# Two transformer layers on one core: the norm's root on another engine, VectorE's exp chain in halves, and other banks for the last MLP groups

## The chip, the core and the metric

The kernel runs on one core of a Trainium2 chip. A core has five engines, each with its own in-order queue: TensorE (matrix multiply, "PE" in the profile, its weight loads "PEld"), VectorE ("DVE"), ScalarE ("ACT"), GpSimd ("POOL") and SyncE ("SP", which here only starts DMAs). They work on the on-chip memory SBUF; TensorE writes its results to PSUM, eight banks of 128 partitions x 512 float32. Engines wait for each other through semaphores. The metric is the device time of one execution in microseconds (us), lower is better. Before the change it is 1762.49 us, the median of three runs (1761.7 to 1763.58).

## The reference

x is 2048 rows of 512 values in bf16. Two layers follow each other, with the same weights:

```
x = x + attention(norm(x)) @ wo        # 32 heads of 16 values, softmax over all 2048 keys
x = x + relu(norm(x) @ w1) @ w2        # w1: 512 x 1792, w2: 1792 x 512
norm(x) = (x - mean) / sqrt(var + 1e-5)
```

The attention makes 2 x 32 x 2048 x 2048 exponentials. That is 4096 blocks of 128 keys x 512 queries, and every element of them has to pass through an engine once or more.

## The kernel before

The program is written out in full by Python code that plans it: the code keeps a clock of its own for TensorE (`now_pe`), VectorE (`now_dve`) and the exponentials (`exp_end`), with constants for the cost of each operation, and by these decides in which order instructions are put into the engines' queues. Once written, the order is fixed.

**Attention.** The main loop (L1048 to 1197) makes one slot after another, 1366 in all. In a slot TensorE makes scores of three blocks (L1147) into one of two PSUM tiles `ps_s` of three banks each, and ScalarE takes the exponential of the whole tile in one instruction (L1156) into one of five buffers `e`. Later TensorE multiplies `e` with the values (`pv`, L835) and sums in the bank `ps_o`. So two slots are in flight: one tile is filled while the other is read. A segment is one head of each of four groups of partitions, for one chunk of queries; at its end VectorE copies `ps_o` out (L739, L758 or L760), and the division by the softmax sums follows over small DMAs and a broadcast `r` that GpSimd's queue starts (L787).

**Blocks that VectorE takes.** In some slots ScalarE takes only two blocks, and the third goes to VectorE, which works out the exponential from the bits of the float. Such blocks come in pairs, two slots apart. For each half VectorE does a first step that reads the scores from PSUM into `di` (L881, `first_step`, put ahead of other work as a "must"). When both halves are there, `chain` (L904) queues five steps on the pair together, 128 x 1024 elements each: `bits` into `dm`, three times `step` (L912: add a constant to one input, multiply by the other), and `bits` into `di` (L906). Then TensorE takes up the three parts of the result (`emit_pair`). At most two pairs may be open (L1071). The chain's steps have the lowest rank among VectorE's tasks (`run_dve`, L323): musts first, then the copies out of the one bank `ps_f`, then other tasks, then chain steps.

**The rest of the layers** is cut into groups that TensorE runs between slots, at a pace that the planner works out from what is left: projections for keys, values and queries, the output projection (`o_group`, L588), the MLP (`h_group`, L613; `z_group`, L644). All of these go through one bank, `ps_f` (`bank()`, L188), which VectorE empties (relu of the MLP: L622). Only before and after the main loop (`wide`) are seven banks used. w1 is loaded tile by tile into four buffers (`load_w1`, L603), four tiles ahead; each load is issued on SP when a group has used its buffer.

**The norm.** `ln_rows` (L485) queues, for a chunk of four (at the end two) row tiles, the statistics (L438, L439), then four tasks of `ln_rstd` (L441), then `ln_apply` (L468), which needs the last of them; TensorE turns the result over (`ln_transpose`) and VectorE copies it out (L513). The four tasks find 1 / sqrt(var + eps) for all rows of the chunk at once, on tiles of 128 x 4 elements: the first makes a start value from the bits of the float (L446, L449, L453), each of the other three is one Newton step of three instructions (L458, L461, L462). The planner counts 600 ns for each task. There are 15 norms of this kind; the first norm of all and the last one are written out directly (L963, L1235) and keep `ln_rstd`.

**The end.** When the last slots are done, `run_all` (L379) puts in whatever groups are left, and then a hand-written last stage (L1202 to 1297) does the last chunk of 256 rows with all banks.

Of the kernel before, what the change touches and what calls it, by code (L numbers as in the profile page):

```python
# [14 lines left out]
ACTF = mybir.ActivationFunctionType  # L15
ALU = mybir.AluOpType
# [6 lines left out]
def kernel(  # L23
# [10 lines left out]
    nc = tc.nc  # L34
# [28 lines left out]
    LEAD, C2, C1, C0 = 0.43216083424908747, -0.036015386827967774, 0.769178243088122, 0.36146642138144963  # L63
# [8 lines left out]
    FLOOR = 0.56  # L72
    C_LAG, R_LAG, U_LAG = 3600.0, 10500.0, 3000.0
    VLAG = 1
    AHEAD = (8.0, 8.0)
    LATE = 0.0
    MID = 2
# [44 lines left out]
    htp = [sb([P, 2, QS], BF16, f"ht{n}") for n in range(NF // 2)]  # L122
    ht = [htp[ft // 2][:, ft % 2, :] for ft in range(NF)]
    ot = [sb([P, QS], BF16, f"ot{t}") for t in range(NT)]
    dm = sb([P, 2, QS], FP32, "dm")
    dy = sb([P, 2, QS], FP32, "dy")
# [18 lines left out]
    va_ = [sb([P, TPC], FP32, f"va{n}") for n in range(2)]  # L145
    ya_ = [sb([P, TPC], FP32, f"ya{n}") for n in range(2)]
    ta_ = [sb([P, TPC], FP32, f"ta{n}") for n in range(2)]
    warm = sb([P, 1], FP32, "warm")

    ps_s = [psum.tile([P, W, QS], FP32, name=f"ps_s{n}") for n in range(2)]  # L150
    ps_o = psum.tile([P, QS], FP32, name="ps_o")
    ps_f = psum.tile([P, QS], FP32, name="ps_f")
# [31 lines left out]
    wide = [True]  # L184
    bank_no = [0]
    in_bank = [None]

    def bank():  # L188
        if not wide[0]:
            return ps_f[:]  # L190
        n = bank_no[0] % 7
        bank_no[0] += 1
        in_bank[0] = (2, 0) if n == 6 else (n // W, n % W)
        if n == 6:
            return ps_f[:]
        return ps_s[n // W][:, n % W, :]
# [26 lines left out]
    def mark(key, engine="dve", lag=0.0):  # L223
        made[key] = (engine, (now_pe if engine == "pe" else now_dve)[0] + lag)
# [34 lines left out]
    def task(cost, fn, makes=(), deps=(), place=None):  # L259
        t = {"cost": cost, "fn": fn, "makes": makes, "deps": deps}  # L260
        dve_q.insert(len(dve_q) if place is None else place, t)
        maker.update({k: t for k in makes})
# [60 lines left out]
    def run_dve(until, musts):  # L323

        while True:
            can = [(0, m[1], m) for m in musts[:1]]
            if now_dve[0] < until:
                can += [(1, e[1], None) for e in list(evac)[:1]]
                for t in dve_q:
                    ready = at(t["deps"], "dve")  # L330
                    if ready is not None:
                        can.append((3 if "chain" in t else 2, ready, t))
            if not can:
                return
            soon = [c for c in can if c[1] <= now_dve[0] + 40.0]
            kind, ready, x = min(soon, key=lambda c: c[0]) if soon else min(can, key=lambda c: c[1])
            if kind and ready >= until:
                if not musts:
                    return
                kind, ready, x = can[0]  # L340
            if kind == 0:
                musts.pop(0)
                dve_run(x[0], x[1])
                x[2]()
            elif kind == 1:
                do_evac()
            else:
                do_task(x)
# [30 lines left out]
    def run_all():  # L379
        while True:  # L380
            finish_group()
            g = next(
                (g for q in (urgent, work) for g in q if at(g["deps"], "pe") is not None), None
            )
            if g is not None:
                start_group(g)
            elif dve_q:
                do_task(next(t for t in dve_q if at(t["deps"], "dve") is not None))
            else:
                break  # L390
        assert not (urgent or work)
# [39 lines left out]
    def ln_n(tag):  # L431
        return ln_seq.index(tag) % 2
# [8 lines left out]
    def ln_rstd(tag, part):  # L441

        n = ln_n(tag)
        a, y, t1 = va_[n], ya_[n], ta_[n]
        if part == 0:
            nc.vector.tensor_scalar(  # L446
                out=a[:], in0=mv[n][:, :, 1], scalar1=EPS, scalar2=None, op0=ALU.add
            )
            nc.vector.tensor_scalar(  # L449
                out=t1[:].bitcast(I32), in0=a[:].bitcast(I32), scalar1=1, scalar2=None,  # L450
                op0=ALU.logical_shift_right,
            )
            nc.vector.tensor_scalar(  # L453
                out=y[:].bitcast(I32), in0=t1[:].bitcast(I32), scalar1=-1.0,
                scalar2=float(RSQRT_SEED), op0=ALU.mult, op1=ALU.add,
            )
            return
        nc.vector.scalar_tensor_tensor(  # L458
            out=t1[:], in0=y[:], scalar=-0.5, in1=y[:], op0=ALU.mult, op1=ALU.mult
        )  # L460
        nc.vector.tensor_mul(out=t1[:], in0=t1[:], in1=a[:])  # L461
        nc.vector.scalar_tensor_tensor(  # L462
            out=y[:], in0=t1[:], scalar=1.5, in1=y[:], op0=ALU.add, op1=ALU.mult
        )

    def ln_apply(tag, tt, i):
        n = ln_n(tag)
        nc.vector.tensor_scalar(  # L468
            out=xnbuf[i][:], in0=x_t[tt][:],
            scalar1=mv[n][:, i, 0:1], scalar2=ya_[n][:, i : i + 1],  # L470
            op0=ALU.subtract, op1=ALU.mult,
        )
# [12 lines left out]
    def ln_rows(tag, tt, n, i):  # L485

        if tag not in ln_seq:
            ln_seq.append(tag)
        prev = ln_seq[ln_seq.index(tag) - 1]
        if ("st", tag, i) not in made:  # L490
            task(860, lambda: ln_stats(tag, tt + i, i), [("st", tag, i)])
        if i == n - 1:
            for part in range(4):
                task(
                    600, lambda part=part: ln_rstd(tag, part), [("rs", tag, part)],
                    [("rs", tag, part - 1)] if part else each(n, "st", tag),
                )
            for k in range(n):
                task(
                    420, lambda k=k: ln_apply(tag, tt + k, k), [("xn", tag, k)],  # L500
                    [("xT", prev, k), ("rs", tag, 3)],
                )
# [20 lines left out]
    def each(n, *key):  # L523
        return [key + (i,) for i in range(n)]
# [88 lines left out]
    def h_group(l, j, ft, war):  # L613
        n = (l * NQS + j) * NF + ft
        _, a, w = columns(l, j)

        number = QS // w
        fts = range(ft, ft + number)
        made_here = [("h", l, j, f) for f in fts]

        def fin(b):
            nc.vector.tensor_scalar(  # L622
                out=htp[ft // 2][:, ft % 2 : ft % 2 + number, a : a + w],
                in0=b.rearrange("p (f q) -> p f q", f=number),
                scalar1=0.0, scalar2=None, op0=ALU.max,
            )
            for key in made_here:
                mark(key)

        def after():  # L630
            for f in range(number):
                load_w1(n + f + NW1)

        return mm_group(
            [
                (w1buf[(n + f) % NW1][:, c, :], xn2T[:, c, a : a + w])
                for f in range(number) for c in range(NDC)
            ],
            fin, made_here,
            each(w // P, "xnT", ("ln2", l, j)) + war + [("w1", n + f) for f in range(number)],  # L640
            after=after, wide_by=w, sums=number,
        )
# [64 lines left out]
    for l in range(2):  # L707
# [11 lines left out]
        for j, Ts, a, b in steps:  # L719
            for T in Ts:  # L720
                sums = acc[8 * j :] if l else acc0
# [182 lines left out]
    def chain(key, di, de):  # L904
        def bits(out, keep, put):
            nc.vector.tensor_scalar(  # L906
                out=out[:].bitcast(I32), in0=di[:].bitcast(I32), scalar1=keep,
                scalar2=put, op0=ALU.bitwise_and, op1=ALU.bitwise_or,
            )

        def step(out, x, c, y):
            nc.vector.scalar_tensor_tensor(  # L912
                out=out[:], in0=x[:], scalar=c, in1=y[:], op0=ALU.add, op1=ALU.mult
            )

        steps = (
            (690, lambda: bits(dm, 0x007FFFFF, 0x3E800000)),
            (1260, lambda: step(dy, dm, C2, dm)),
            (1260, lambda: step(dy, dy, C1, dm)),
            (1260, lambda: step(de, dy, C0, di)),  # L920
            (690, lambda: bits(di, 0x7F800000, KAPPA_BITS)),
        )
        for n, (cost, fn) in enumerate(steps):
            k = key + (n,) if n + 1 < len(steps) else key
            task(cost, fn, [k], [key + (n - 1,)] if n else [])
            maker[k]["chain"] = True
# [271 lines left out]
    while pend:  # L1198
        emit_pv()
        run_dve(0.0, musts)  # L1200
    run_all()
    wide[0] = True  # L1202
    users.clear()
    l, j = 1, NQS
    tag = ("ln2", l, j)
# [122 lines left out]
```

The softmax here doesn't subtract the row's maximum and nothing guards it: scores larger than these inputs give would overflow.

## Time and profile before

| | |
|---|---|
| time, median of three runs | 1762.49 us |
| time of the profiled run, its span | 1761.06 us, 1759.3 us |
| ScalarE: exponentials (L1156) | 1366 instructions, 1695.6 us |
| VectorE: pairs | 166: first steps (L881) 332 x 687 ns; `step` (L912) 498 x 1.21 to 1.22 us; `bits` (L906) 332 x 0.69 us |
| VectorE: Newton steps (L458, L461, L462) | 3 x 51 instructions, 160 to 162 ns each |
| TensorE: scores (L1147) | 8100 matmuls, 761.5 us |
| VectorE: relu of the MLP (L622) | 105 instructions, 687 ns each |
| granted TensorE clock | 0.998 of full speed |

A profile is of one execution. A group's row has the line, the engine, the operation, its tiles and shapes, how often it ran, the busy time in us and the mean ns of one; behind the second bar stands how long the engine was idle just before such instructions, and whom it waited for. In the lists of waits the three numbers are the total in us, how many, and the longest. In the timeline each row has the start and the length in us, and in brackets the idle time before it with the engine and line that ended it; equal instructions that follow each other are merged. Consecutive instructions of one engine may overlap a little in these records, so a sum of durations can be more than the time from the first start to the last end.

### The profile page before, as it was taken

To read this page: it belongs to the slowest core of one execution; us is meant where nothing else is said; L and a number is where in the kernel's file an instruction comes from. 1 tells how busy PE (TensorE), PEld (TensorE's weight loads), DVE (VectorE), ACT (ScalarE), POOL (GpSimd) and SP (SyncE) were. 2 spreads that over 40 slices of the span, in tenths; PEclk is the share of its full clock that TensorE was granted. 3 is DMA by queue.
4 is the path that set the end of the run, shared out by engine and by line. 5 is a ranking of instruction groups with operands and counts; after the bars stand their busy time and mean duration, and the time that the engine had idled before them with its cause. 6 is when DMAs were issued, how large, how long until landed. Compare 5 with 4: busy or idle time off the path is not lost.

```text
span 1759.3 us, 35344 instructions
## 1 busy us (share of the span) xinstructions
PE 1643.2 (93%) x15404; PEld 533.1 (30%) x15404; DVE 1481.9 (84%) x2250; ACT 1706.0 (97%) x1386; POOL 35.5 (2%) x80
## 2 busy tenths in 40 slices
PE   8998889999999999999999999999999999999997
PEld 3222222222222222222222222222222222454454
DVE  7437889999899899899798997889988888888883
ACT  7999999999999999999999999999999999999991
POOL 0000000000000000000000000000000000000000
PEclk9999999999999999999999999999999999999999
DMA  4000000110002000021000100000110011011103
GB/s 150 1 1 2 2 2 14 35 28 14 2 17 43 17 14 8 11 43 23 8 1 7 28 10 1 3 3 17 37 21 22 9 41 29 17 21 36 27 18 84
DMA packets 104268, 38.10 MB, mean 22 GB/s; under 512 B 93713, under 2 KB 101649, under 8 KB 104113
## 3 DMA queue, kind: packets, MB, share of 16 engines
q1 hardware_dynamic: 92192, 24.38, 6.0%
q0 software_dynamic: 10576, 10.16, 3.1%
q8 instruction: 120, 1.97, 0.5%
q10 hardware_dynamic: 1344, 1.31, 0.2%
q14 instruction: 36, 0.29, 0.1%
HBM read 22.54 MB, written 2.10 MB: 14 GB/s over the span
## 4 chain that ended last, share of the span: by engine, by line
ACT 82%; PE 12%; DVE 3%; issue 2%; DMA 1%; SPq 0%; ACTq 0%
ACT e L1156 82%; PE ps_s L1147 4%; PE ps_f L409 4%; PE ps_o L835 3%; DVE dy L912 1%; PE ps_s L1222 1%; DVE ht L622 1%; DMA wqkv<-in_A_wqkv_dram 0%; DVE di L881 0%; DVE de L912 0%; DVE u L760 0%; PE ps_f L1222 0%; DMA x<-in_A_x_dram 0%; PE ps_s L980 0%; DVE stats L438 0%
## 5 line engine op out<-in xcount | busy, mean ns | idle before, releaser
L1156 ACT ACTIVATE e<-ps_s 128x1536 bf16<-128x1536 f32 (+1 forms) x1366 | 1695.6, 1458 | 5.4 <-PE ps_s L1147 4.8
L1147 PE MATMUL ps_s<-q,ktp 32*128 32x512 bf16 (+1 forms) x8100 | 761.5, 355 | 86.4 <-ACT e L1156 71.5
L835 PE MATMUL ps_o<-e,vaug 128*32 128x512 bf16 (+1 forms) x4230 | 428.9, 363 | 3.0 <-DVE u L758 1.1
L1147 PEld LDWEIGHTS <-ktp 32*128 32x128 bf16 x8100 | 243.2, 92 | 605.9 <-issue 498.7
L881 DVE TENSOR_SCALAR di<-ps_s 128x512 int32<-128x512 f32 x332 | 228.1, 687 | 83.9 <-PE ps_s L1147 81.5
L835 PEld LDWEIGHTS <-vaug 128*32 128x32 bf16 x5364 | 146.2, 94 | 304.9 <-issue 279.2
L912 DVE SCALAR_TENSOR_TENSOR dy<-dm 128x1024 f32<-128x1024 f32 x166 | 202.6, 1220 | 4.1
L912 DVE SCALAR_TENSOR_TENSOR dy<-dy,dm 128x1024 f32<-128x1024 f32 x166 | 201.8, 1216 | 2.0
L912 DVE SCALAR_TENSOR_TENSOR de<-dy,di 128x1024 bf16<-128x1024 f32 x166 | 201.2, 1212 | 1.1
L409 PE MATMUL ps_f<-xn2T,w 128*128 128x512 bf16 (+1 forms) x448 | 121.4, 370 | 4.7 <-DVE ht L622 4.7
L835 PE MATMUL ps_o<-de,vaug 128*32 128x512 bf16 (+1 forms) x756 | 112.2, 356 | 5.7 <-DVE u L760 2.4
L906 DVE TENSOR_SCALAR di<-di 128x1024 int32<-128x1024 int32 x166 | 113.7, 685 | 2.7
L906 DVE TENSOR_SCALAR dm<-di 128x1024 int32<-128x1024 int32 x166 | 114.0, 686 | 0.6
L409 PE MATMUL ps_f<-w,ht 128*128 128x512 bf16 x392 | 113.9, 383 | 0.1
L409 PE MATMUL ps_f<-xnT,wqkv 128*128 128x512 bf16 (+1 forms) x312 | 91.5, 374 | 2.5 <-DVE ktp L530 1.2
L622 DVE TENSOR_SCALAR ht<-ps_f 128x512 bf16<-128x512 f32 x105 | 72.1, 687 | 23.0 <-PE ps_f L409 22.0
L570 DVE TENSOR_SCALAR q<-ps_f,qmask 128x512 bf16<-128x512 f32 (+1 forms) x94 | 62.9, 699 | 24.2 <-PE ps_f L409 23.7
L409 PE MATMUL ps_f<-wo,ot 128*128 128x512 bf16 x240 | 69.6, 383 | 1.0 <-DVE x L593 1.0
L835 PE MATMUL ps_o<-di,vaug 128*32 128x512 bf16 (+1 forms) x378 | 70.5, 363 | 0.0
L787 POOL DMA_DIRECT2D r<-u x45 | 33.1, 736 | 1663.5 <-DVE di L881 558.8
L409 PEld LDWEIGHTS <-w 128*128 128x128 bf16 x448 | 34.2, 97 | 74.4 <-issue 58.6
L773 DVE SCALAR_TENSOR_TENSOR ot<-u,mask,r 128x512 bf16<-128x512 f32 (+2 forms) x74 | 49.4, 672 | 1.0
(85 smaller groups left out, 553.0 us busy)
## 6 DMA issues: line engine op xcount, KB each, us to landing
w<-in_B_w_dram SPq DMA_DIRECT2D x126, 128.0 KB
r<-u POOLq DMA_DIRECT2D x32, 256.0 KB, 7.1
out_dram<-x SPq DMA_DIRECT2D x16, 128.0 KB
x<-in_A_x_dram SPq DMA_DIRECT2D x14, 128.0 KB
w<-in_B_w_dram SPq DMA_DIRECT2D x1, 1792.0 KB
r<-u POOLq DMA_DIRECT2D x13, 128.0 KB, 4.5
wqkv<-in_A_wqkv_dram ACTq DMA_DIRECT2D x2, 512.0 KB
c<-u SPq DMA_DIRECT2D x56, 8.0 KB
```

The source lines that it names most:

```text
L409: nc.tensor.matmul(out, lhsT, rhs, start=i % k == 0, stop=i % k == k - 1)
L570: return nc.vector.tensor_scalar(out=qbuf[n % 2][e][:, 0:w], in0=b, scalar1=qmask[e][:, 0:1], scalar2=None, op0=ALU.mult,)
L622: nc.vector.tensor_scalar(out=htp[ft // 2][:, ft % 2 : ft % 2 + number, a : a + w], in0=b.rearrange("p (f q) -> p f q", f=number), scalar1 ...
L773: nc.vector.scalar_tensor_tensor(out=ot[t][:, at_column + a : at_column + a + w], in0=u[:, a : a + w], scalar=mask[e][:, 0:1], in1=r[:, a ...
L787: nc.gpsimd.dma_start(out=r[:, 0:width], in_=bass.AP(tensor=sums.tensor, offset=sums.offset, ap=[list(sums.ap[0]), [0, 32], [1, width]],),)
L835: nc.tensor.matmul(ps_o[32 * g : 32 * g + 32, 0 : sg["w"]], vaug[sg["l"]][kb][:, 4 * sg["T"] + g, 2 * e : 2 * e + 32], rhs, start=g not in ...
L881: first = nc.vector.tensor_scalar(out=di[:, half, :].bitcast(I32), in0=src, scalar1=EXP_BIAS, scalar2=0.0, op0=ALU.add, op1=ALU.max,)
L906: nc.vector.tensor_scalar(out=out[:].bitcast(I32), in0=di[:].bitcast(I32), scalar1=keep, scalar2=put, op0=ALU.bitwise_and, op1=ALU.bitwise_or,
L912: nc.vector.scalar_tensor_tensor(out=out[:], in0=x[:], scalar=c, in1=y[:], op0=ALU.add, op1=ALU.mult)
L1147: nc.tensor.matmul(b[:, a : a + sg["w"]], kt[32 * g : 32 * g + 32, kc : kc + P], qbuf[sg["n"] % 2][sg["e"]][32 * g : 32 * g + 32, 0 : sg[" ...
L1156: ex = nc.scalar.activation(out=eb[:, 0 : place[m]], in_=b[:, 0 : place[m]], func=ACTF.Exp, scale=1.0 / (LOG2E * UNIT),)
L1222: uses(nc.tensor.matmul(out, lhsT, rhs, start=first, stop=last), b, needs=needs)
```

## The change

Three edits are made together.

1. *The norm's root.* Where `ln_rows` queued four tasks, it queues one. It makes the start value on VectorE as before (`ln_rstd(tag, 0)`) and then issues the three Newton steps on GpSimd (`ln_newton`), four instructions a step, twelve in all, each of which needs the one before. The planner counts 600 ns of VectorE for it, and takes the result to be there 5000 ns later (`RSTD_LAG`).
2. *The chain of a pair.* Each of the three `step` instructions on 128 x 1024 elements becomes two on 128 x 512, first half and second half in turn. The planner counts 660 ns for each instead of 1260 ns for the whole. `bits` stays as it is.
3. *The groups left at the end.* While `run_all` puts in what is left after the last slot (`ending`), `bank()` goes around three banks, `ps_f` and the first bank of each `ps_s`, and the MLP's relu is done by ScalarE instead of VectorE.

```diff
+    RSTD_LAG = 5000.0
...
     def bank():
+        if ending[0]:
+            bank_no[0] += 1
+            return (ps_f[:], ps_s[0][:, 0, :], ps_s[1][:, 0, :])[bank_no[0] % 3]
         if not wide[0]:
             return ps_f[:]
...
+    def ln_newton(tag):
+
+        n = ln_n(tag)
+        a, y, t1 = va_[n][:], ya_[n][:], ta_[n][:]
+        for _ in range(3):
+            nc.gpsimd.tensor_mul(out=t1, in0=y, in1=y)
+            nc.gpsimd.tensor_mul(out=t1, in0=t1, in1=a)
+            nc.gpsimd.tensor_scalar(
+                out=t1, in0=t1, scalar1=-0.5, scalar2=1.5, op0=ALU.mult, op1=ALU.add
+            )
+            nc.gpsimd.tensor_mul(out=y, in0=y, in1=t1)
...
-            for part in range(4):
-                task(
-                    600, lambda part=part: ln_rstd(tag, part), [("rs", tag, part)],
-                    [("rs", tag, part - 1)] if part else each(n, "st", tag),
-                )
+
+            def rstd():
+                ln_rstd(tag, 0)
+                ln_newton(tag)
+                mark(("rs", tag, 3), lag=RSTD_LAG)
+
+            task(600, rstd, [("rs", tag, 3)], each(n, "st", tag))
...
+            if ending[0]:
+                nc.scalar.activation(out=out, in_=sums, func=ACTF.Relu)
+            else:
+                nc.vector.tensor_scalar(
+                    out=out, in0=sums, scalar1=0.0, scalar2=None, op0=ALU.max
+                )
...
-            (1260, lambda: step(dy, dm, C2, dm)),
-            (1260, lambda: step(dy, dy, C1, dm)),
-            (1260, lambda: step(de, dy, C0, di)),
+            (660, lambda: step(dy[:, 0], dm[:, 0], C2, dm[:, 0])),
+            (660, lambda: step(dy[:, 1], dm[:, 1], C2, dm[:, 1])),
+            (660, lambda: step(dy[:, 0], dy[:, 0], C1, dm[:, 0])),
+            (660, lambda: step(dy[:, 1], dy[:, 1], C1, dm[:, 1])),
+            (660, lambda: step(de[:, 0], dy[:, 0], C0, di[:, 0])),
+            (660, lambda: step(de[:, 1], dy[:, 1], C0, di[:, 1])),
...
+    ending[0] = True
     run_all()
-    wide[0] = True
+    ending[0], wide[0] = False, True
```

More of the change, by code (lines that the diff above doesn't have):

```diff
@@ L186 @@
     in_bank = [None]
+    ending = [False]
     def bank():
+        if ending[0]:
+            bank_no[0] += 1
+            return (ps_f[:], ps_s[0][:, 0, :], ps_s[1][:, 0, :])[bank_no[0] % 3]
         if not wide[0]:
@@ L621, in fin @@
         def fin(b):
[L622 to L626, printed above, removed]
+            out = htp[ft // 2][:, ft % 2 : ft % 2 + number, a : a + w]
+            sums = b.rearrange("p (f q) -> p f q", f=number)
+            if ending[0]:
[4 more added lines that the diff above has]
+                )
             for key in made_here:
@@ L912, in step @@
             nc.vector.scalar_tensor_tensor(
-                out=out[:], in0=x[:], scalar=c, in1=y[:], op0=ALU.add, op1=ALU.mult
+                out=out, in0=x, scalar=c, in1=y, op0=ALU.add, op1=ALU.mult
             )
```

## The prediction

> **What bounds the kernel now.** I read the page from the top (busy shares, then the chain that ended last), then the groups with shapes kept apart, the waits, and last the timeline of the end.
>
> ```profile
> PE 1643.2 (93%) x15404; PEld 533.1 (30%) x15404; DVE 1481.9 (84%) x2250; ACT 1706.0 (97%) x1386; POOL 35.5 (2%) x80
> ACT 82%; PE 12%; DVE 3%; issue 2%; DMA 1%; SPq 0%; ACTq 0%
> ```
>
> ScalarE is busy for 97% of the span and makes 82% of the last chain. GpSimd does nearly nothing. In the groups:
>
> ```profile
> L1156 ACT ACTIVATE e<-ps_s 128x1536 bf16<-128x1536 f32 x1033 | 1456.2, 1563 | 3.6 <-PE ps_s L1147 3.1
> L1156 ACT ACTIVATE e<-ps_s 128x1024 bf16<-128x1024 f32 x332 | 374.5, 1136 | 1.8 <-PE ps_s L1147 1.7
> L881 DVE TENSOR_SCALAR di<-ps_s 128x512 int32<-128x512 f32 x332 | 228.1, 687 | 83.9 <-PE ps_s L1147 81.5
> L912 DVE SCALAR_TENSOR_TENSOR dy<-dm 128x1024 f32<-128x1024 f32 x166 | 202.6, 1220 | 4.1
> ```
>
> The exponentials run from 16.66 us to 1717.3 us. From start to start in the trace, one of three blocks takes 1.330 us at the median, one of two 0.904 us: a block that VectorE takes saves ScalarE 0.426 us, a pair 0.85 us. At these medians the 1366 exponentials would take 1673.7 us from first start to last; they take 1700.0. So 26.3 us are lost in late scores, though the idle column shows only 5.4 us (an exponential overlaps the next, so a late start hides in it). The span is 16.7 us of start, 1673.7 of exponentials, 26.3 of lateness, and 42 us from the last exponential to the end. Each edit must change one of these four, or the number of pairs (166).
>
> Who makes scores late? The waits:
>
> ```profile
> PE ps_s L1147 <- ACT e L1156: 71.5, 217, 0.7
> PE ps_o L835 <- DVE u L760: 3.2, 7, 0.9
> PE ps_s L1147 <- DVE di L881: 2.4, 5, 0.8
> ```
>
> TensorE waits mostly for ScalarE itself. All its waits for VectorE between 150 and 1717 us add to some 15 us. Going back from each exponential over 60 ns late to the last wait of TensorE before it, 5.6 of the 26.3 us follow a wait for VectorE. The end:
>
> ```profile
> 1719.48 1.03 PE L409 MATMUL ps_f<-xn2T,w 128*128 128x256 bf16 x8 [0.78 <-DVE ht L622]
> 1719.48 0.75 PEld L409 LDWEIGHTS <-w 128*128 128x128 bf16 x7 [0.96 <-issue]
> 1720.55 0.69 DVE L622 TENSOR_SCALAR ht<-ps_f 128x512 bf16<-128x512 f32 x1 [1.12 <-PE ps_f L409]
> 1720.60 0.10 PEld L409 LDWEIGHTS <-w 128*128 128x128 bf16 x1 [0.37 <-DMA w<-in_B_w_dram]
> 1721.30 1.03 PE L409 MATMUL ps_f<-xn2T,w 128*128 128x256 bf16 x8 [0.78 <-DVE ht L622]
> ```
>
> Seven MLP groups stand behind the last exponential, from 1717.65 to 1729.58: eight matmuls, then TensorE waits 0.78 us for VectorE to empty the one bank, 1.82 us a group. The weight load of the group after next has only just landed (fourth line).
>
> **What the skill says.** *SBUF — State Buffer*, "Who interferes with whom": a VectorE instruction with two SBUF inputs, or in a 2-port mode, excludes a GpSimd instruction that reads SBUF, and the reverse; the later one waits for the whole of the other. The chain's steps (L912) have two SBUF inputs. No row of before shows GpSimd arithmetic, so the trace neither confirms nor denies it. *VectorE: DVE Perf Modes*, "The DRAIN you can't avoid": the next instruction waits until the pipe is empty. The trace differs: where the next doesn't depend on the one before, it starts 0.083 us before that one's end; where it does, 0.034 us after. The measurement decides. *ScalarE: Activation LUTs*, "Table sets": relu is in every set, so no table load; the trace agrees (Exp, Relu and copies, one ACT_TABLE_LOAD).
>
> **The change, part by part.**
>
> *Newton.* Nine VectorE instructions leave each of 15 norms, 0.196 us from start to start: 1.76 us each. Three lie before 50 us, where VectorE is idle enough; 12 lie among the pairs: 21 us. In the planner's costs it is 1800 ns, 21.6 us in 12 norms. GpSimd gets 12 dependent instructions. Bounds for one: below, the 0.122 us of GpSimd's memset (1.5 us in all); above, a whole half step in front of each, 0.68 + 0.12 us (9.6 us). I take 0.36: 0.12 of its own, 0.05 for the semaphore, and 0.19 for the lock (chain work is about 4.9 of the 9.4 us from pair to pair, 166 in 1556 us, and the mean rest of a half step 0.34 us). That is 4.3 us, under the 5.0 us the planner leaves, so normally hidden by the chain work placed between. Where it isn't, xn (L468) waits at the head of VectorE's in-order queue, behind it first steps, copies and evacuations, and behind these TensorE. GpSimd's queue also carries the 45 broadcasts r (L787, 0.7 us each, waiting for small DMAs), behind one of which Newton may stand, and which may stand behind Newton. I take +0.5 us in all, bounds 0 and +14.
>
> *Half steps.* A 128x1024 step takes 1.22 us, 1.067 of it for the elements at 0.96 per ns, so 0.153 is fixed; a half step is estimated at 0.686 (an addition of 128x512 f32, L758, takes 0.682). Alternating halves don't depend on the instruction just before, so each should cost 0.60: six make 3.61 us. Now three make 3.52 (1.216 each, less 0.043, the mean of the two kinds of gap as counted). So +0.09 us a pair, 15 us, which the 21 us from Newton cover. In the planner's costs a chain rises from 5160 to 5340: 180 ns x 166 = 29.9 us. Net for the plan: 29.9 - 21.6 = 8.3 us more VectorE work, at 6720 a pair 1.2 pairs fewer: +1.0 us. (The plan is limited by VectorE: in the timeline a chain begins as the last ends, and only two pairs may be open.) Bounds: 5 pairs either way, since the order is replanned, 4.3 us each way. The gain: a copy or first step that arrives during a chain step waits at the mean half of it, 0.34 instead of 0.61 us, 44% less. Of the 5.6 us of lateness behind VectorE: -2.5 us; bounds 0 and -5.6.
>
> *The end.* With three banks TensorE no longer waits for the evacuation. ScalarE has been idle there since 1717.3; its relu of 128x512 at about 0.6 us (a copy takes 0.585) fits beside a group. But w1 has four buffers, two per group: the load into group 2's first buffer, started when it had been read, released the weights of group 4 at 1722.40, 2.92 us after group 2 began at 1719.48. So two groups can't take less than 3.0 us. Starts at 0, 0.9, 3.0, 3.9, 6.0, 6.9, 9.0, end at 10.0 instead of 11.9: -1.9 us. Bounds 0 and -5.6 (seven at 0.9). VectorE's own last steps, now free early, gain nothing: TensorE's 17 matmuls from 1729.42 fill the time to ScalarE's copy at 1733.29. Against it: the norm just before. Its Newton ends at 1712.92, its transposes run at 1714.13 and 1715.00, and the second copy is done at 1715.88, 1.77 us before the first MLP group. Without chains there GpSimd's Newton takes 2 to 4 us instead of 1.77, which that slack hides; but the plan puts xn 3.2 us later (600 + 5000 against 4 x 600), perhaps behind the last exponential, where two transposes and a copy cost some 1.6 us. I take half, +0.8; bounds 0 and +3.
>
> Sum: +0.5 + 1.0 - 2.5 - 1.9 + 0.8 = -2.1 us, from 1759.3 to 1757.2 of span. The profiled run's time was 1761.06; the other runs' median is 1762.49, 3.2 above the span, so **1760.4 us**.
>
> **Rivals.** *The replanned order holds more pairs.* For: two chains in flight are the limit, and smaller steps let evacuations in sooner, so chains may start sooner. Against: the planner's VectorE cost rises by 8.3 us. Six more pairs: -5.1 us instead of +1.0, at 1754.3; I say 1755.
>
> *GpSimd is late* (slower). Place: xn after each of 12 norms in the full stretch. Point from which it decides: 5.0/12 = 0.42 us for one GpSimd instruction. At 0.8 us Newton takes 9.6; VectorE stands still after 5 us, with half the instructions left, which alone then take some 0.2 to 0.4 us each, 1.2 to 2.5 us. Scores have about one exponential, 1.3 us, in hand, so up to 1.2 us each reaches ScalarE, 12 to 14 us in all: 1772. For: more than half of VectorE's time holds the lock. Against: first steps and evacuations read PSUM and leave gaps.
>
> *The plan loses pairs.* Five fewer instead of 1.2: +3.3 us, at 1764 to 1766.
>
> *It does nothing at the end:* w1 loads are the limit, or the norm comes late: 1.9 us back, 1762.3, within my case.
>
> **How the numbers follow.** My case 0.50, its own range 1756.5 to 1764; more pairs 0.25; GpSimd late 0.17; fewer pairs 0.08. The range 1753 to 1768 leaves out the worse half of the late case and the best of the second, under 2 in 10. About 0.2%, 3.5 us, is what a measurement can tell from no change, so faster means under 1759.0 and slower over 1766.0. Faster: 0.17 of my case and 0.24 of more pairs, 0.41. Slower: 0.16 and 0.04, 0.20. Within: 0.39.
>
> **What would show it.** Right: L912 at 0.68 to 0.69 us x996; exponentials of two blocks within four of 332; TensorE's waits for VectorE copies nearly halved; GpSimd's Newton under 5 us and no VectorE wait for POOL at L468; groups in the end alternating 0.9 and 2.1 us apart, released by w1's DMAs. Wrong: VectorE idle before L468 on POOL by over 1 us a norm; half steps at 0.72 us apart (then 6 x 0.12 us x 166 = 120 us of VectorE are missing, more than its idle time bears); two-block exponentials off by more than ten.

## The result, and the profile after

The changed kernel takes 1754.18 us (median of four runs, 1753.1 to 1754.77) against 1762.92 us for the kernel before beside it: a ratio of 0.9951, 95% interval 0.9933 to 0.9968. It is faster by 0.5%. The profiled span went from 1759.3 to 1751.9 us. The page begins:

```profile
PE 1649.5 (94%) x15476; PEld 529.7 (30%) x15476; DVE 1477.8 (84%) x2589; ACT 1708.9 (98%) x1390; POOL 98.7 (6%) x260
...
ACT 87%; PE 8%; DVE 3%; issue 1%; DMA 1%
```

ScalarE is still what carries the chain, and with a larger share: 87% instead of 82. What shrank is TensorE's share (12% to 8%). Most of it lies ahead of the last exponential, where the chain is on TensorE for 119.5 us instead of 188.6; behind it the chain is on TensorE for 23.2 us instead of 27.6. The groups, shapes kept apart:

```profile
L1182 ACT ACTIVATE e<-ps_s 128x1536 bf16<-128x1536 f32 x1037 | 1462.7, 1574 | 1.4 <-PE ps_s L1173 1.1
...
L1182 ACT ACTIVATE e<-ps_s 128x1024 bf16<-128x1024 f32 x328 | 373.9, 1150 | 1.5 <-PE ps_s L1173 1.5
...
L904 DVE TENSOR_SCALAR di<-ps_s 128x512 int32<-128x512 f32 x328 | 225.7, 689 | 88.6 <-PE ps_s L1173 83.5
...
L935 DVE SCALAR_TENSOR_TENSOR dy<-dm 128x512 f32<-128x512 f32 x328 | 213.7, 684 | 3.8
...
L486 DVE TENSOR_SCALAR xn<-x,mv,ya 128x512 bf16<-128x512 bf16 x64 | 23.0, 407 | 7.0 <-POOL ya L482 6.7
```

There are 164 pairs, two fewer: VectorE takes less work from ScalarE, not more. A half step takes 0.684 us, as estimated. The last row has the new wait: xn stood for GpSimd for 6.7 us in all. The waits of TensorE:

```profile
PE ps_s L1173 <- ACT e L1182: 64.7, 196, 0.8
...
DVE xn L486 <- POOL ya L482: 6.7, 5, 2.3
...
PE ps_o L858 <- DVE u L783: 2.7, 8, 0.6
```

The copies of ps_o (last row) let TensorE wait for 2.7 us instead of 3.2: the wait that half steps were to shorten has hardly changed. The end, from the timeline:

```profile
1702.67 0.41 DVE L533 COPY xn2T<-ps_f 128x512 bf16<-128x512 bf16 x1
...
1716.40 1.05 PE L415 MATMUL ps_f<-xn2T,w 128*128 128x256 bf16 x8
...
1717.28 1.04 PE L415 MATMUL ps_s<-xn2T,w 128*128 128x256 bf16 x8
...
1717.48 0.60 ACT L645 ACTIVATE ht<-ps_f 128x512 bf16<-128x512 f32 x1 [1.45 <-PE ps_f L415]
...
1719.25 1.28 PE L415 MATMUL ps_s<-xn2T,w 128*128 128x256 bf16 x8 [0.93 <-DMA w<-in_B_w_dram]
...
1720.56 1.20 PE L415 MATMUL ps_f<-xn2T,w 128*128 128x256 bf16 x8
```

Here is most of the gain. The last exponential ends at 1716.03. The last copy of the norm before the MLP ends at 1703.08, 13 us before that. Before the change the last exponential ended at 1717.29 and that copy 1.4 us ahead of it:

```profile
1715.46 0.42 DVE L513 COPY xn2T<-ps_f 128x512 bf16<-128x512 bf16 x1 [0.47 <-PE ps_f L477]
```

So three of the seven groups have already run between the slots, and four are left. These follow each other at 0.88, 1.97 and 1.31 us; what holds the third is no longer VectorE but the DMA of its weights.

The four terms of the prediction (start to first exponential; exponentials at the median pace; lateness of scores; end), in us from the trace. The pace is that of the kernel before in both columns, 1.330 us for three blocks and 0.904 us for two:

| | before | after | difference |
|---|---|---|---|
| start | 16.7 | 17.4 | +0.7 |
| exponentials at pace | 1673.7 | 1675.4 | +1.7 |
| lateness | 26.3 | 22.4 | -3.9 |
| last exponential to the end | 42.0 | 35.8 | -6.2 |

The sum is -7.7 us; the span has -7.4, the rest is rounding and the length of the last exponential itself. The changed kernel's own median for two blocks is 0.913 us; by that, 3.0 us more would stand under pace and 3.0 less under lateness.

### The profile page after: what moved, and what is told of

Read it like the earlier page. It is cut to its first block, busy times and chain, and to the rows that moved or that the text cites. A ratio compares the mean times of both kernels' runs of the same rounds, so it can differ in the third digit from the quotient of the medians.

```text
span 1751.9 us, 36000 instructions
## 1 busy us (share of the span) xinstructions
PE 1649.5 (94%) x15476; PEld 529.7 (30%) x15476; DVE 1477.8 (84%) x2589; ACT 1708.9 (98%) x1390; POOL 98.7 (6%) x260
## 3 DMA queue, kind: packets, MB, share of 16 engines
q10 hardware_dynamic: 1344, 1.31, 0.2%
## 4 chain that ended last, share of the span: by engine, by line
ACT 87%; PE 8%; DVE 3%; issue 1%; DMA 1%
ACT e L1182 87%; PE ps_s L1173 2%; PE ps_f L415 2%; PE ps_o L858 2%; PE ps_s L1249 1%; DVE di L904 0%; DVE de L935 0%; DVE stats L444 0%; DMA u<-c 0%; DVE dy L935 0%; DMA x<-in_A_x_dram 0%; PE ps_f L1249 0%; PE ps_s L1006 0%; DVE dm L929 0%; DVE u L783 0%
## 5 line engine op out<-in xcount | busy, mean ns | idle before, releaser
L1173 PE MATMUL ps_s<-q,ktp 32*128 32x512 bf16 (+1 forms) x8184 | 771.8, 357 | 78.5 <-ACT e L1182 64.7
L935 DVE SCALAR_TENSOR_TENSOR dy<-dm 128x512 f32<-128x512 f32 x328 | 213.7, 684 | 3.8
L935 DVE SCALAR_TENSOR_TENSOR dy<-dy,dm 128x512 f32<-128x512 f32 x328 | 216.8, 681 | 0.0
L935 DVE SCALAR_TENSOR_TENSOR de<-dy,di 128x512 bf16<-128x512 f32 x328 | 215.9, 681 | 0.0
L810 POOL DMA_DIRECT2D r<-u x45 | 33.3, 740 | 1282.7 <-DVE di L904 493.4
L444 DVE BATCH_NORM_STATS2 stats<-x 128x6 f32<-128x512 bf16 x64 | 43.7, 683 | 9.1 <-ACT x L1259 6.0
```

The source lines that it names most:

```text
L444: nc.vector.bn_stats(out=st[:], in_=x_t[tt][:])
L810: nc.gpsimd.dma_start(out=r[:, 0:width], in_=bass.AP(tensor=sums.tensor, offset=sums.offset, ap=[list(sums.ap[0]), [0, 32], [1, width]],),)
L935: nc.vector.scalar_tensor_tensor(out=out, in0=x, scalar=c, in1=y, op0=ALU.add, op1=ALU.mult)
L1173: nc.tensor.matmul(b[:, a : a + sg["w"]], kt[32 * g : 32 * g + 32, kc : kc + P], qbuf[sg["n"] % 2][sg["e"]][32 * g : 32 * g + 32, 0 : sg[" ...
```

## The experiments

Each was timed beside the kernel before on the same chip. The experiments ran on three chips, so the ratios are what can be compared. "Left" counts the MLP groups that were not finished at the end of the last exponential, and "end" is the time from there to the end of the profiled span. Two columns show what goes with them: "norm" is when the last copy of the norm ahead of these groups ended, from the end of the last exponential, and "half" for how many us TensorE's granted clock was at half among the exponentials. "Lateness" is reckoned with the pace of the kernel before in all rows. All of these but the first two columns are from one profiled execution each.

| | time, us | ratio to before (95%) | pairs | lateness | half | norm | left | end |
|---|---|---|---|---|---|---|---|---|
| before | 1762.9 | 1 | 166 | 26.3 | 6.8 | -1.4 | 7 | 42.0 |
| after | 1754.2 | 0.9951 (0.9933 to 0.9968) | 164 | 22.4 | 0 | -13.0 | 4 | 35.8 |
| E1 end alone | 1761.4 | 0.9996 (0.9987 to 1.0005) | 166 | 26.6 | 6.8 | -1.4 | 7 | 41.9 |
| E2 half steps alone | 1753.9 | 0.9953 (0.9941 to 0.9965) | 163 | 21.8 | 0 | -12.1 | 4 | 36.5 |
| E3 Newton alone | 1782.4 | 1.0111 (1.0098 to 1.0124) | 167 | 33.3 | 0 | +6.1 | 7 | 55.2 |
| E4 without the end | 1755.6 | 0.9955 (0.9943 to 0.9967) | 164 | 22.4 | 0 | -12.9 | 4 | 37.0 |
| E5 without Newton | 1754.7 | 0.9952 (0.9939 to 0.9964) | 163 | 23.3 | 3.4 | -12.1 | 4 | 35.3 |
| E6 half steps, old order | 1762.6 | 0.9999 (0.9991 to 1.0006) | 166 | 26.9 | 6.8 | -1.4 | 7 | 42.0 |
| E7 whole steps, E2's order | 1756.5 | 0.9961 (0.9949 to 0.9973) | 163 | 23.0 | 0 | -12.1 | 4 | 36.5 |
| E8 E3's order, Newton on VectorE | 1796.8 | 1.0192 (1.0174 to 1.0209) | 167 | 49.7 | 23.9 | +7.1 | 7 | 55.5 |
| E9 half steps at 630 | 1749.9 | 0.9932 (0.9918 to 0.9945) | 165 | 23.1 | 3.4 | -20.2 | 2 | 32.4 |
| E10 whole steps at 1320 | 1787.8 | 1.0143 (1.0125 to 1.0161) | 163 | 38.8 | 27.3 | +5.6 | 7 | 54.3 |
| E11 E8 with 1800 ns lag | 1804.2 | 1.0237 (1.0224 to 1.0250) | 170 | 53.9 | 27.3 | +12.0 | 7 | 60.2 |
| E12 E5, six w1 buffers | 1753.1 | 0.9946 (0.9934 to 0.9958) | 163 | 21.8 | 0 | -12.1 | 4 | 34.1 |

The granted clock is a rival to every small difference here. Each run has its mean clock on record, to three digits, and one and the same kernel is, as a rule, slower in runs with a lower mean: the kernel before took 1759.4 to 1760.5 us in its four runs at 0.999 of full speed, 1761.0 to 1762.1 in fifteen at 0.998, and 1763.1 to 1765.1 in twelve at 0.996. So some pairs are also compared at one clock (mean times in us; in brackets how many runs):

| | clock | the one | the other | difference |
|---|---|---|---|---|
| after, before | 0.999 | 1754.8 (2) | 1759.9 (4) | -5.1 |
| E1, before | 0.998 | 1759.8 (5) | 1761.5 (15) | -1.6 |
| E6, before | 0.998 | 1762.1 (8) | 1761.5 (15) | +0.6 |
| E2, E7 | 0.999 | 1755.4 (1) | 1756.5 (5) | -1.1 |
| E4, after | 1.000 | 1754.2 (2) | 1753.4 (2) | +0.9 |
| E12, E5 | 0.999 | 1753.1 (1) | 1754.6 (2) | -1.5 |
| E9, after | 0.999 | 1749.2 (2) | 1754.8 (2) | -5.6 |

These are few runs, in part on different chips, and the clock is rounded, so a difference under 1 us says little. But some 5 of the 8.7 us stay at the same clock. The rest goes with the clock, and the clock seems to go with the order: in the old order (before, E1, E6) the runs of the experiments lie at 0.994 to 0.999, in those of E2 and of the changed kernel at 0.998 to 1.000.

### Which edit makes the gain? (E1 to E4)

The theory after the first look: the groups that were already done make most of it, and the half steps brought them forward. The rivals: the end's banks alone, or Newton. E1 has only the hunks of `bank()`, `fin` and `run_all` (the last is shown):

```diff
...
+    ending[0] = True
     run_all()
-    wide[0] = True
+    ending[0], wide[0] = False, True
```

> The kernel before with the third edit alone (three banks and ScalarE's relu while the left-over groups run). Theory 'earlier work' (most of the gain at the end comes from MLP groups that the new order had already done before the last exponential): the order up to the last exponential is that of before, so seven groups stay behind it; at the pace of w1's loads they take some 10.0 us instead of 11.9, so about -1.9 us, 1761.0. Rival 'banks': the end's banks alone make most of the gain, -5 us or more, 1758 or less.

Measured: 1761.35, a ratio of 0.9996 that can't be told from 1. In its timeline the seven groups keep the pace of the prediction's sum to the end (starts at 0, 0.9, 3.0, 4.1, 6.0, 7.1, 9.0); the first four:

```profile
1718.07 1.05 PE L414 MATMUL ps_f<-xn2T,w 128*128 128x256 bf16 x8
...
1718.95 1.04 PE L414 MATMUL ps_s<-xn2T,w 128*128 128x256 bf16 x8
...
1721.10 1.15 PE L414 MATMUL ps_s<-xn2T,w 128*128 128x256 bf16 x8 [1.12 <-DMA w<-in_B_w_dram]
...
1722.19 1.18 PE L414 MATMUL ps_f<-xn2T,w 128*128 128x256 bf16 x8
```

Two groups in 3.0 us, and the stage after them starts 10.4 us after the last exponential instead of 12.1. But in the profiled execution the end as a whole is no shorter (41.9 us): the last stage takes 31.5 us instead of 29.9, and TensorE's clock is at half for 3.4 us in it, where before it was not. The windows have the stretch, its length, the busy time of PE, PEld, DVE, ACT and POOL, and last the granted clock, the share of the DMA engines and GB/s:

```profile
1728.00:1737.00 9.00, 7.36 (x35) 3.24 (x34) 3.87 (x17) 2.25 (x4) 0.00 (x0) 1.00 0.16 38
1737.00:1742.00 5.00, 4.39 (x22) 2.47 (x24) 1.32 (x4) 0.97 (x2) 0.00 (x0) 0.66 0.20 52
```

So the rival "banks", which asked for 5 us or more, falls. The 1.7 us lie inside the interval of the ratio; at the same clock they are seen (-1.6 us, all five runs faster than any of the fifteen).

E2 has only the step hunk of the change (six tasks of 660).

> The kernel before with the second edit alone (chain in half steps, 660 each in the plan). Theory 'earlier work, by half steps': evacuations wait less behind a chain step in the plan, so MLP groups get through the one bank sooner; about four groups instead of seven stay behind the last exponential (-5.5 us at 1.82 us each), lateness of the exponentials falls from 26 to some 22 us, two to five pairs fewer (+0.85 us each): 1755 to 1760. Rival 'Newton': half steps alone lose pairs and gain nothing at the end: 1763 to 1766, seven groups left.

Measured: 1753.93, four groups left, a little under the expected range. The second edit alone makes the whole gain. E3 has only the first edit, `ln_newton` and `RSTD_LAG`:

> The kernel before with the first edit alone (Newton steps on GpSimd, 5000 ns later in the plan). Theory 'earlier work, by half steps': the groups left stay at six to eight, VectorE's freed 21 us give one to three pairs more, xn waits for GpSimd 1 us at some norms: 1760 to 1764. Rival 'Newton': it is VectorE's freed time that brings the work forward: four groups left, 1756 to 1758.

Measured: 1782.36, 1.1% slower, which neither theory had. Two things are seen in its timeline. First, the lock:

```profile
1721.90 1.22 DVE L927 SCALAR_TENSOR_TENSOR dy<-dm 128x1024 f32<-128x1024 f32 x1
...
1722.08 1.10 POOL L472 TENSOR_TENSOR ta<-ya 128x4 f32<-128x4 f32 x1 [13.74 <-DVE ya L454]
...
1723.15 1.22 DVE L927 SCALAR_TENSOR_TENSOR dy<-dy,dm 128x1024 f32<-128x1024 f32 x1
...
1723.25 1.18 POOL L473 TENSOR_TENSOR ta<-ta,va 128x4 f32<-128x4 f32 x1
...
1724.41 1.22 DVE L927 SCALAR_TENSOR_TENSOR de<-dy,di 128x1024 bf16<-128x1024 f32 x1
...
1726.49 0.20 POOL L472 TENSOR_TENSOR ta<-ya 128x4 f32<-128x4 f32 x1
```

A GpSimd instruction on 4 elements lasts 1.10 to 1.18 us while VectorE is in a whole step, and 0.20 us when VectorE is idle; each of the long ones ends 0.06 us after the step. Second, this norm is the last one: its result comes behind the last exponential (1725.12), TensorE has little to do, and its clock falls to half for 20.5 us (the third column from the end). In it eight matmuls take 1.87 us instead of 1.03 and a group 2.65 us instead of 1.82:

```profile
1725.00:1729.00 4.00, 1.10 (x17) 0.54 (x13) 2.07 (x4) 0.12 (x1) 2.90 (x10) 1.00 0.00 0
1729.00:1733.00 4.00, 2.49 (x16) 1.68 (x17) 1.26 (x4) 0.00 (x0) 0.00 (x0) 0.75 0.00 0
1733.00:1738.00 5.00, 3.44 (x16) 2.15 (x15) 1.38 (x2) 0.00 (x0) 0.00 (x0) 0.50 0.46 105
```

These make up the longer end: the first group starts 5.8 us later after the last exponential than before, the seven groups take 5.8 us more, and the last stage 1.6, of 13.2 us in all. Most of the rest of the loss is lateness, 7.0 us.

E4 is the changed kernel without the hunks of E1:

> The changed kernel without the third edit. The order up to the last exponential is that of the changed kernel, four groups left. Theory 'earlier work': these go through one bank at 1.82 us each, from the first start to the next stage 6.5 us instead of 5.2 to 5.5, so 1.0 to 1.5 us slower than the changed kernel: about 1755.5. Rival 'banks': 4 us or more slower, 1758 or more.

Measured: 1755.57, as "earlier work" had it. The difference of its ratio to that of the changed kernel is within both intervals; at the same clock it is 0.9 us.

### Is it VectorE's queue, or the order? (E5 to E8)

E5 leaves out only Newton's hunk:

> The changed kernel without the first edit: half steps and the end's banks. If the edits add up where they don't meet (half steps alone 1753.9; the end's banks 1.2 us between the run without them, 1755.6, and the changed kernel, 1754.2), it takes 1752.5 us, faster than the changed kernel. Rival: Newton on GpSimd is worth something once the steps are halves, then this is 1755 or more.

Measured: 1754.68. The hoped-for 1752.5 isn't there; with half steps, Newton on GpSimd can't be told from Newton on VectorE.

E6 and E7 separate the two things that a half step is: an instruction half as long, and a task half as long in the plan. E6 has the instructions without the tasks:

```diff
-            (1260, lambda: step(dy, dm, C2, dm)),
+            (1260, lambda: both(dy, dm, C2, dm)),
...
+        def both(out, x, c, y):
+            for h in range(2):
+                step(out[:, h], x[:, h], c, y[:, h])
```

> The kernel before; each of the chain's three steps is issued as two half steps, but directly behind each other as one task of 1260 in the plan, so that the order of all else is that of before. Theory 'order' (half steps gain because the planner orders the work anew): seven groups left, lateness 25 to 27 us, 1761 to 1763. Rival 'engine' (half steps gain because VectorE's queue itself moves sooner): lateness 22 us or less, 1757 to 1759.

E7 has the tasks without the instructions:

```diff
-            (660, lambda: step(dy[:, 0], dm[:, 0], C2, dm[:, 0])),
-            (660, lambda: step(dy[:, 1], dm[:, 1], C2, dm[:, 1])),
+            (660, lambda: None),
+            (660, lambda: step(dy[:], dm[:], C2, dm[:])),
...
```

> The order of the half-step kernel (second edit alone), but with whole steps: of two tasks of 660 the first issues nothing and the second issues the step on 128x1024. Theory 'order': about four groups left at the end, 163 pairs, 1754 to 1757. Rival 'engine': the order alone brings nothing, lateness is back at 26 us and VectorE is late for the groups: 1759 or more.

Measured: E6 1762.62, nothing gained, lateness 26.9; E7 1756.5, four groups left, lateness 23.0. E7's end:

```profile
1717.08 1.05 PE L409 MATMUL ps_f<-xn2T,w 128*128 128x256 bf16 x8
1718.91 1.03 PE L409 MATMUL ps_f<-xn2T,w 128*128 128x256 bf16 x8 [0.78 <-DVE ht L622]
1720.72 1.03 PE L409 MATMUL ps_f<-xn2T,w 128*128 128x256 bf16 x8 [0.78 <-DVE ht L622]
1722.54 1.03 PE L409 MATMUL ps_f<-xn2T,w 128*128 128x256 bf16 x8 [0.78 <-DVE ht L622]
1723.41 0.38 PE L1225 MATMUL ps_s<-x,ident 128*128 128x512 bf16 x1
```

The traces show the orders as intended: up to the last exponential ScalarE's instructions, and VectorE's other than the steps, follow each other in E6 as before the change, and in E7 as in E2. The order makes most of the gain, with whole steps too. The shorter instruction adds little, and only in the new order: E2 is 1.1 us faster than E7 at the same clock (at 1.000 too), with 1.2 us less lateness, and TensorE waits for VectorE for 10.6 us between 150 and 1710 us instead of 16.1 (before 15.4, E6 15.7). Their ratios (0.9953 and 0.9961) have overlapping intervals.

Halves do cost VectorE the little that was worked out. From the start of a step to the start of the next instruction E6 takes 1.20 us at the median where that doesn't depend on the step, against 1.14 before (329 times), and 1.21 against 1.25 where it does (169 times). That is some 14 us in all, and 15 were estimated.

E8 takes E3's order and issues Newton on VectorE in the same place:

```diff
-                ln_newton(tag)
+                for part in range(1, 4):
+                    ln_rstd(tag, part)
```

> The order of the kernel with the first edit alone (1782.4 us), but the Newton steps are issued on VectorE in the same place. Theory 'lock' (that loss comes from GpSimd waiting for VectorE's whole steps: Newton 5.5 to 7 us instead of 3.3 free, and from TensorE's clock at half after its idle at the end): no wait for GpSimd, full clock at the end, 1762 to 1768. Rival 'lag' (the loss is in the plan, which takes the root 5000 ns later): 1776 or more.

Measured: 1796.83, 14 us slower than E3. So "lock" does not carry the loss: without GpSimd the run is slower still, and its last norm too comes behind the last exponential (7.1 us; in E3 6.1). E8 is not a clean test of what the lock costs, since it also gives VectorE work that the plan doesn't count; in E3 xn waited for GpSimd for 11.0 us in all.

### Grain or chance? (E9 to E12)

Every edit to a cost gives another order, so E2 might have been luck. E9 puts the half steps at 630, so that a chain costs the plan what it did before; E10 puts whole steps at 1320, so that it costs what the halves cost:

```diff
-            (1260, lambda: step(dy, dm, C2, dm)),
+            (1320, lambda: step(dy, dm, C2, dm)),
...
```

> The kernel before with half steps alone, each counted as 630 in the plan, so that a chain costs the plan what it did (5160). Theory 'grain' (it is the finer grain of the plan's steps that brings the MLP groups forward): four or five groups left, 1752 to 1757, as with 660. Rival 'chance' (any other cost gives another order, and 660 happened to give a good one): as likely six to eight groups left, 1759 to 1766.

> The kernel before with whole steps, each counted as 1320 instead of 1260: the plan's cost of a chain is that of the half steps (5340), the grain is not. Theory 'grain': no gain, six to eight groups left, some five pairs fewer, 1762 to 1768. Rival 'cost' (the larger cost, so fewer pairs, leaves room for the groups): 163 pairs, four groups left, 1754 to 1757. Rival 'chance': anything from 1755 to 1780.

Measured: E9 1749.92, two groups left, the first of them half done; E10 1787.79, seven left. Both lie outside all that was expected, E9 below and E10 above, and only the number of groups in E10 is as "grain" had it. E9's end:

```profile
1716.68 1.03 PE L409 MATMUL ps_f<-xn2T,w 128*128 128x256 bf16 x8 [0.78 <-DVE ht L622]
...
1717.75 0.69 DVE L622 TENSOR_SCALAR ht<-ps_f 128x512 bf16<-128x512 f32 x1 [1.12 <-PE ps_f L409]
...
1721.42 1.08 ACT L1235 CAST x<-ps_s 128x512 bf16<-128x512 f32 x2 [6.49 <-PE ps_s L1225]
```

The second of the two groups, still through one bank, and the last stage follows. In E10, as in E3, the norm comes behind the last exponential and the groups run at half clock:

```profile
1740.57 1.87 PE L409 MATMUL ps_f<-xn2T,w 128*128 128x256 bf16 x8 [0.78 <-DVE ht L622]
...
1743.22 1.87 PE L409 MATMUL ps_f<-xn2T,w 128*128 128x256 bf16 x8 [0.78 <-DVE ht L622]
```

E10 has as many pairs as E2 (163), so fewer pairs is not what helped: the rival "cost" falls. All three orders that were planned with half steps (630; 660; 660 with Newton) have two to four groups left and a lateness of 22 to 23 us; all four planned with whole steps (1260; 1320; that of E3 and E8; that of E11) have seven and 26 to 54. That speaks for "grain", but seven orders are few, and "chance" is not excluded. How the grain would do it was not shown.

The column "norm" says what to ask next. Seven is all the groups that need the last norm. In the orders with whole steps its last copy ends 1.4 us ahead of the last exponential at best, so all seven are left whatever VectorE does later; in those with half steps it ends 12 to 20 us ahead. So what differs is how early the plan gets this norm done, and no run changed that alone.

E11 sets `RSTD_LAG` to 1800 in E8:

> The run with Newton's order on VectorE (whole steps, 1796.8 us), with the root taken 1800 ns later in the plan instead of 5000, about what VectorE needs for it. Theory 'lag' (the loss is that the plan takes the root 5000 ns later): near the kernel before, 1760 to 1767. Rival 'count' (the loss is that 1800 ns of each norm aren't counted as VectorE's work, so that it lags behind the plan) or 'chance': 1775 or more.

Measured: 1804.18, worse still, so "lag" falls as well. It has 170 pairs, so 3.4 us less than before for the exponentials at their pace (1670.3 us), and loses far more in lateness (53.9 us instead of 26.3). That fits "count" (1800 ns a norm that VectorE does and the plan doesn't know of), but it isn't shown: TensorE's clock at half for 27.3 us among the exponentials adds to the lateness, and "chance" expected the same time. E3 and E10, which have no such work, are slow without it, so the cause of their orders is open.

E12 is E5 with `NW1 = 6`:

> The changed kernel without its first edit (1754.7 us), with six w1 buffers instead of four. If w1's loads set the pace of the groups left at the end (2.85 us for two), six buffers let three groups run at TensorE's pace, 0.9 us, and four groups take some 4 us instead of 5.5: -1.5 us, 1753 us, if the order stays. Rival: loads aren't what holds them, no change at the end.

Measured: 1753.07. The stage after the groups begins 4.2 us after the last exponential instead of E5's 5.5, so w1's loads were what held them. By the ratios the time can't be told from E5's; at the same clock it is 1.5 us shorter, as expected.

E9 beats the kernel before clearly (0.9932). Against the changed kernel its median is 4 us lower, and at the same clock 5.6 us, but the two weren't timed beside each other, and their intervals against before overlap by a little.

## Why the prediction was right or wrong

The direction was right and the range held (1753 to 1768), near its edge. The forecast was 1760.4, 2.1 us faster; it was 8.7 us. That the range held was luck: my own case ended at 1756.5, and the lower part was there for the rival "more pairs", named at 1755. The time came out near that, but there are two pairs fewer, not six more.

- **Pairs:** 1.2 fewer, +1.0 us. Measured two fewer, +1.7. Right.
- **Lateness:** -2.5 us, because what arrives at VectorE would wait for half a step less. Measured -3.9, for the most part not for that reason: E6 has the short steps and none of it, E7 has long steps and most of it. This step failed: it took a duration from VectorE's queue where the order was what counts. What short steps are worth in the new order is some 1.1 us (E2 against E7). Most of the fall goes with the clock. In the kernel before, TensorE's clock is at half from 197 to 200 us and from 238 to 241 us, and the two largest gaps of ScalarE among the exponentials (0.64 and 0.60 us) lie there. The first stretch (the last columns are the granted clock, the share of the DMA engines and GB/s):

```profile
196.00:198.00 2.00, 1.48 (x15) 0.49 (x11) 1.97 (x2) 2.00 (x2) 0.00 (x0) 0.69 0.00 0
198.00:201.00 3.00, 3.00 (x19) 0.54 (x13) 1.64 (x2) 1.97 (x3) 0.00 (x0) 0.64 0.00 0
```

  Of the 26.3 us, 2.5 arise from 2 us ahead of these two stretches to 3 us behind them. The changed kernel's trace has no such stretch during the exponentials, and of its fall in lateness only some 1.4 us lie elsewhere. The order alone doesn't set these stretches: E2, E5 and E12 share one order up to the last exponential, and only E5 has one, with 1.5 us more lateness than the other two.
- **Newton:** 0.36 us an instruction and 4.3 us in all. Measured, in the norms of the full stretch: 0.52 to 0.65 us behind half steps, 0.20 free (0.28 from start to start), and 4.7 to 6.2 us in all, where the plan has 5. The lock was mis-sized: I let an instruction wait for half of a step on the mean, and only for the share of time that the chain holds, but one that is issued beside a chain waits for nearly a whole step, as the steps follow without a gap. In two of the twelve norms the first instruction also stood 1.6 and 2.6 us behind a broadcast r in GpSimd's queue, which the prediction had named. xn stood 6.7 us in all, where no such wait was named as the sign of being right; it stays that small since GpSimd is fast again as soon as VectorE stands. The rival "GpSimd late" decided from 0.42 us an instruction; the mean of 12 came to 0.39 to 0.52 and cost nothing that can be measured.
- **The end's pace:** starts at 0, 0.9, 3.0, 3.9. Measured 0, 0.88, 2.85, 4.16, and in E1 0, 0.88, 3.03, 4.12. Right.
- **The end's content:** this is the term that failed most. I kept seven groups behind the last exponential, and even let the norm move later (+0.8). Measured: three of the seven were gone, and the end is 6.2 us shorter instead of 1.1. I had written that "the order is replanned", and used that for the number of pairs alone. The same freedom moves the work at the end, where one group is worth 1.82 us and a norm that comes too late some 13 us (E3).
- **A reading of the skill:** the prediction sets the trace against *VectorE: DVE Perf Modes*, "The DRAIN you can't avoid". That section goes on to say that a next instruction that isn't held starts earlier, so the overlap of 0.083 us doesn't contradict it.

## What to carry to other kernels

Where a planner writes out the order, a change to the cost or the grain of one task has to be read first as a new order: put the new plan on the old instructions, and the old plan on the new ones, before any duration is held responsible. Compare runs at the same granted clock before a difference of a few us is explained. Count what is left behind the last instruction of the bounding engine; it shows at once what such a change does. Small dependent work on GpSimd beside VectorE is priced by VectorE's instruction length, so shorten that first, and leave the waiting instruction room.

## What was not expected of the hardware

- GpSimd's arithmetic on 128x4 f32 takes 0.19 to 0.20 us, start to start 0.28, if VectorE leaves it alone; beside half steps 0.5 to 0.65 us, beside whole steps up to 1.18 us. VectorE's own step stays at 1.22 us beside it. *SBUF — State Buffer*, "Who interferes with whom", has the exclusion; these runs show it for a `scalar_tensor_tensor` with two SBUF inputs.
- In E3 TensorE is busy for 1.10 us of the 4.0 from 1725 us, and for 0.79 of the next 2.0. From 1731.0 its clock is at half for 20.5 us, although matmuls fill 3.44 of 5.0 us in it, and the groups take 2.65 us instead of 1.82. That the idle time brings this on was not tested, but the three other runs with a norm behind the last exponential (E8, E10, E11) have the same, for 23.9 us. Shorter stretches at half, of 3.4 to 13.7 us, occur in the middle of the exponentials; E2, E7 and the changed kernel have none there.
- For one kernel on one core, 0.001 of mean granted clock goes with some 1.5 us of 1760: the kernel before took 1759.9 us on the mean at 0.999, 1761.5 at 0.998, 1762.9 at 0.997 and 1764.6 at 0.996.
